# The output of the last pass is turned by VectorE in squares of 32 instead of by TensorE

## The chip, the core and the metric

The kernel runs on one core of a Trainium2 chip. The engines are TensorE (PE; its weight loads are listed as PEld), VectorE (DVE), ScalarE (ACT), GpSimd (POOL) and SyncE (SP), which issues most DMA transfers. The metric is the device time of one execution in microseconds; of before there are three runs.

## The reference

Linear attention with a softmax on both sides, and then two feed-forward blocks on its 4608 x 512 output. All inputs are float32, or float64 in the weights.

```python
q_s = softmax of q over its last axis; k_s = softmax of k over the sequence
kv  = einsum('bhsd,bhse->bhde', k_s, v)
x   = einsum('bhsd,bhde->bhse', q_s, kv)          # (8, 8, 576, 64)
x   = x.transpose(0, 2, 1, 3).reshape(4608, 512)
h   = x @ w_in;  g = h / (1 + exp(-1.702 h));      x   = g @ w_out
h   = x @ w2_in; g = h, (h + 1)**2 / 4 or 0;       out = g @ w2_out
```

The last product, g (4608 x 2048) by w2_out (2048 x 512), is the last pass of the kernel, and the one that the change is about.

## The kernel before, in words

**Products.** All four matrix products run on PE in three parts each: an operand is split into a rounded part (hi, line 107, by ACT) and the remainder (lo, line 108, by DVE), and a product is the sum of hi by hi, hi by lo and lo by hi. The last three matrix products are also cut into 2 x 2 blocks and done with seven block products instead of eight, numbered in the order `PROD = (1, 7, 6, 2, 5, 4, 3)`. Their block operands are sums of quadrants, formed by DVE (`operand` and `last_sum`, through the helper on line 121).

**The last pass** is `out_pass` with `ph = 1`. Activations stand with features on the partitions and tokens along the columns. The tokens are cut into five groups (`HALVES`); a group has two halves of 512 columns (the first three groups) or 384 (the last two). For each group and each of the seven products there are four steps i (a quarter of the sum over features); a step is 12 matmuls of 128 x 512 or 128 x 384 (line 344). `ready(s)` makes hi and lo of step s; the loop calls it three steps ahead (`LA = 3`). hi and lo rotate through seven buffers, so those of step s + 3 take the place of what step s reads.

**The end of a product** is `post`. Three PSUM tiles of two banks hold running sums: "a" (products 1 and 2), "p" (7 and 4) and "x" (a copy of the first, then 6, 5 and 3). After 1 ACT copies a to x (line 420); after 7 and 6 it copies the sum to buffers s7 and u2 (`keep`, line 407); after 2 and 3 it copies the finished blocks c11 and c12. After 5 and 4, DVE adds the sum to s7 and u2 (`more`). Each finished block is 256 output features by 512 or 384 tokens.

**Turning.** The output wants tokens on rows, so a block must be turned. `store` puts it in a list, and `turn`, called after step i = 2 of the next product, does it: eight PE transposes of 128 columns (line 367) into the fourth PSUM tile, a copy to SBUF by ACT (line 376), and one transfer whose runs in the output are 256 floats, 1 KB (line 378). The very last product is run in two halves of its output features; `close` copies each half (lines 390 and 392), and the second half is turned after the last matmul (lines 373 and 374).

**What sets the order.** Each engine takes its instructions in one fixed order. A scheduler in the framework sets it ahead of time, from its own estimates; `behind(x, y)` pins x after y on one engine without a wait. The loads of the next group's quadrants (`Quadrants.load`, line 267) are issued by SP after products 2, 5 and 4 and stand in one queue with the outputs. Quadrant "22" of the next group, loaded after product 4, is first read by the sums for product 7.

Of the kernel before, what the change touches and what calls it, by code (L numbers as in the profile page):

```python
# [8 lines left out]
FP32 = mybir.dt.float32  # L9
# [9 lines left out]
def kernel(  # L19
# [11 lines left out]
    nc = tc.nc  # L31
# [72 lines left out]
        return first  # L104

    def split(hi, lo, src):
        nc.scalar.activation(out=hi, in_=src, func=ACTF.Copy)  # L107
        return nc.vector.tensor_tensor(out=lo, in0=src, in1=hi.bitcast(FP32), op=ALU.subtract)  # L108


    def behind(ins, other):
# [12 lines left out]
    def weight_sets(width, raws, f12, f_r, f_s, hls):  # L124
        w_srcs = {"out1": w1_out, "in2": w2_in, "out2": w2_out}
        hl_n = [0]

        def raw(i):
            return raws[i % len(raws)].bitcast(I64)


        def load(w, si, i):
            src = w_srcs[w]
            if w == "in2":
                c0 = i * (DFF // 2) + si * width
# [12 lines left out]
        def convert(i):  # L148
            conv(raw(i), f12[i], f_r.bitcast(U32))

        def quads(w):
            if w == "in2":
                v4 = [f.rearrange("p (k f) -> p k f", k=KD) for f in f12]
                return v4[0][:, 0:2], v4[0][:, 2:4], v4[1][:, 0:2], v4[1][:, 2:4]
            v2 = [f.rearrange("p (c f) -> p c f", c=width // P) for f in f12]
            return v2[0][:, :, 0:256], v2[1][:, :, 0:256], v2[0][:, :, 256:512], v2[1][:, :, 256:512]

        def hl(w, si, p, src, neg=False):
            t = hls[hl_n[0] % len(hls)].bitcast(FP32R)
            hl_n[0] += 1  # L160
            t = t.rearrange("p (a c f) -> p a c f", a=2, c=src.shape[1])
            hi, lo = t[:, 0], t[:, 1]
            if neg:
                nc.scalar.activation(out=hi, in_=src, func=ACTF.Copy, scale=-1.0)
                nc.vector.scalar_tensor_tensor(
                    out=lo, in0=src, scalar=-1.0, in1=hi.bitcast(FP32), op0=ALU.mult, op1=ALU.subtract
                )
            else:
                split(hi, lo, src)
            n = 2 * width  # L170
            dst = wp_dram[w, p].rearrange("p a s f -> p a (s f)")[:, :, si * n:(si + 1) * n]
            nc.sync.dma_start(out=dst, in_=t.bitcast(FP32).rearrange("p a c f -> p a (c f)"))

        def sums(w, si, part):
            a11, a12, a21, a22 = quads(w)
            s = f_s.rearrange("p (c f) -> p c f", c=a11.shape[1])
            if part == 0:
                hl(w, si, 1, a11)
                tt(s, a21, a22, ALU.add)
            elif part == 1:  # L180
                hl(w, si, 5, s)
                hl(w, si, 4, a22, neg=True)
                tt(a21, a11, a21, ALU.subtract)
            elif part == 2:
                tt(s, s, a11, ALU.subtract)
                hl(w, si, 6, s)
                hl(w, si, 2, a12)
            else:
                hl(w, si, 7, a21)
                tt(a12, a12, s, ALU.subtract)  # L190
                hl(w, si, 3, a12)

        return load, convert, sums
# [53 lines left out]

    G_AT = ({"11": 0, "12": 4, "22": 8, "21": 12}, {"11": 0, "12": 16, "22": 4, "21": 12})
    R_AT = ((16, 17, 18, 19, 24, 25, 26), (8, 9, 10, 11, 25, 26, 24))
    O_AT = {"s7": 20, "u2": 21, "c11": 22}  # L250
    C_AT = {p: 4 + 2 * i for i, p in enumerate(PROD)}
    C_AT[PROD[-1]] = 20
    E_AT = (22, 23, 24, 25, 26)
# [46 lines left out]
    def out_pass(ph, gq, sl):  # L300
# [8 lines left out]
        def ready(s):  # L309
            if s >= len(steps):  # L310
                return
            j, p, i = steps[s]
            src, ins = operand(gq.t[j], p, i)
            if j == 0:
                behind(ins, last.get(s - 2))
            n = HALVES[j]
            if ph and s < len(first_at):
                at = first_at[s]
            elif ph and s >= len(steps) - 4:
                at = (i, 16 + i)  # L320
            else:
                k = 2 * (s - len(first_at) * ph)
                at = [r_at[(k + x) % len(r_at)] for x in range(2)]
            hi, lo = (slot(x, FP32R)[:, :, :n] for x in at)
            last[s] = split(hi, lo, src)
            ops[s] = hi, lo
            if p == 2:
                last_sum(gq.t[j], i)

        def gemm(s, ms=range(2)):  # L330
            j, p, i = steps[s]
# [16 lines left out]
                            skip_group_check=True,  # L348
                        )

        late = []

        def store(j, a, b, t):
            n, t0 = HALVES[j], STARTS[j]
            if not ph:
                nc.sync.dma_start(out=x1_dram[j, a, b], in_=t)
            else:
                late.append((j, a, b, t, (0, 1)))

        def turn():  # L360
            for j, a, b, t, ms in late:
                n, t0 = HALVES[j], STARTS[j]
                n4 = n // 4
                pt = bank(2, "pt").rearrange("p a c -> p (a c)").rearrange("p (r d) -> p r d", r=4)
                for r in range(4):
                    for m in ms:
                        nc.tensor.transpose(  # L367
                            out=pt[:n4, r, m * P:(m + 1) * P], in_=t[:, m, r * n4:(r + 1) * n4], identity=ident
                        )
                u = slot(23).rearrange("p a c -> p (a c)").rearrange("p (r d) -> p r d", r=4)  # L370
                d = slice(ms[0] * P, (ms[-1] + 1) * P)
                if ms == (1,):
                    nc.scalar.activation(out=u[:n4, :2, d], in_=pt[:n4, :2, d], func=ACTF.Copy)
                    nc.vector.tensor_copy(out=u[:n4, 2:, d], in_=pt[:n4, 2:, d])
                else:
                    nc.scalar.activation(out=u[:n4, :, d], in_=pt[:n4, :, d], func=ACTF.Copy)
                r0 = t0 + b * n
                nc.sync.dma_start(
                    out=out[r0:r0 + n, a * 256 + d.start:a * 256 + d.stop].rearrange("(r p) d -> p r d", r=4),
                    in_=u[:n4, :, d],  # L380
                )
            late.clear()


        def close(m):
            n = HALVES[-1]
            z = zs["x"][:, m, :n]
            t = tmp["c12"] = tmp["c12"] if m else slot(20)[:, :, :n]
            c = n // 2 if m else n
            nc.scalar.activation(out=t[:, m, :c], in_=z[:, :c], func=ACTF.Copy)  # L390
            if m:
                nc.vector.tensor_copy(out=t[:, m, c:], in_=z[:, c:])
            late.append((NJ - 1, 0, 1, t, (m,)))

        tmp = {}

        def post(j, p):
            n = HALVES[j]
            z = zs[Z_OF[p]][:, :, :n]

            def new(name):
                at = O_AT[name] if name in O_AT else (20 if ph else 23)
                return slot(at)[:, :, :n]

            def keep(name):
                t = new(name)
                nc.scalar.activation(out=t, in_=z, func=ACTF.Copy, scale=1.0 if ph else 0.5)
                return t

            def more(t):  # L410
                if ph:
                    tt(t, t, z, ALU.add)
                else:
                    nc.vector.scalar_tensor_tensor(
                        out=t, in0=z, scalar=0.5, in1=t, op0=ALU.mult, op1=ALU.add
# [1 line left out]

            if p == 1:
                zs["x"] = bank(3, "zx")
                nc.scalar.activation(out=zs["x"][:, :, :n], in_=z, func=ACTF.Copy)  # L420
            elif p == 7:
                tmp["s7"] = keep("s7")
            elif p == 6:
                tmp["u2"] = keep("u2")
            elif p == 2:
                store(j, 0, 0, keep("c11"))
            elif p == 5:
                more(tmp["s7"])
                store(j, 1, 1, tmp["s7"])
            elif p == 4:  # L430
                more(tmp["u2"])
                store(j, 1, 0, tmp["u2"])
            else:
                store(j, 0, 1, keep("c12"))

        LA = 3

        def run(hooks, done, first=()):
# [2 lines left out]
            whole = len(steps) - 4 * ph  # L441
            for s, (j, p, i) in enumerate(steps[:whole]):
                gemm(s)
                if i == 2 and ph:
                    turn()
                if i == 3:
                    post(j, p)
                    if j + 1 < NJ:
# [2 lines left out]
                    else:  # L451
                        for f, a in hooks.get(p, ()):
                            f(*a)
                if s + LA >= done:
                    ready(s + LA)
                if s == 3:
                    for f, a in first:
# [1 line left out]
            if ph:  # L459

                for m in range(2):
                    for i in range(4):
                        gemm(whole + i, (m,))
                        if m == 0 and i == 0:
                            ready(whole + 3)
                        if i == 2:
                            turn()
                    close(m)
                turn()

        return ready, run

# [522 lines left out]
```

## Time and profile before

| | |
|---|---|
| median of three runs | 1594.03 us |
| the three runs | 1591.33, 1594.03, 1594.37 us |
| the profiled execution: span, first to last instruction | 1588.7 us |
| the profiled execution's own device time | not recorded; the median is 5.3 us above the span |
| PE busy | 1555.3 us (98%) |
| DVE busy | 1146.4 us (72%) |
| ACT busy | 850.9 us (54%) |
| last pass | about 1241 to 1588.7 us |
| transposes on PE in the last pass | 160, from 1271.3 to 1584.0 us |
| output transfers | 21 |

The span is what the profiler sees from the first to the last instruction; the device time of a run has a few microseconds more around it. A busy share is an average over stages; the rows further down are of single stages.

### The profile page before, as it was taken

To read this page: it belongs to the slowest core of one execution; us is meant where nothing else is said; L and a number is where in the kernel's file an instruction comes from. 1 tells how busy PE (TensorE), PEld (TensorE's weight loads), DVE (VectorE), ACT (ScalarE), POOL (GpSimd) and SP (SyncE) were. 2 spreads that over 40 slices of the span, in tenths; PEclk is the share of its full clock that TensorE was granted. 3 is DMA by queue.
4 is the path that set the end of the run, shared out by engine and by line. 5 is a ranking of instruction groups with operands and counts; after the bars stand their busy time and mean duration, and the time that the engine had idled before them with its cause. 6 is when DMAs were issued, how large, how long until landed. Compare 5 with 4: busy or idle time off the path is not lost. (4 is left out here: it accounts for less than half of the span.)

```text
span 1588.7 us, 21246 instructions
## 1 busy us (share of the span) xinstructions
PE 1555.3 (98%) x7908; PEld 1324.5 (83%) x7908; DVE 1146.4 (72%) x1519; ACT 850.9 (54%) x1090; POOL 8.8 (1%) x45
## 2 busy tenths in 40 slices
PE   4999999999999999999999999999999999999998
PEld 2677888777778888888999887878999888888998
DVE  6999888788753778686677687868465776766573
ACT  5555545544532444444445787878676444444453
POOL 0000000000000000000000000000000000000000
PEclk9999999999999999999999999999999999999999
DMA  8787888887778661615368766566547853424421
GB/s 229 216 262 258 279 257 270 279 286 249 237 268 302 241 237 54 225 44 169 113 205 330 272 212 246 196 239 226 203 156 285 350 206 112 153 86 134 133 66 41
DMA packets 219272, 330.66 MB, mean 208 GB/s; under 512 B 90144, under 2 KB 163232, under 8 KB 216480
## 3 DMA queue, kind: packets, MB, share of 16 engines
q1 hardware_dynamic: 214688, 328.19, 60.8%
q10 hardware_dynamic: 4480, 1.11, 0.3%
q8 instruction: 62, 1.02, 0.3%
q14 instruction: 42, 0.34, 0.1%
HBM read 190.84 MB, written 138.41 MB: 207 GB/s over the span
## 5 line engine op out<-in xcount | busy, mean ns | idle before, releaser
L107 ACT ACTIVATE s<-s 128x1024 fp32r<-128x1024 f32 (+2 forms) x363 | 325.2, 901 | 363.7 <-PE z L344 171.3
L108 DVE TENSOR_TENSOR s<-s,s 128x1024 fp32r<-128x1024 f32 (+2 forms) x363 | 369.9, 1024 | 162.5 <-PE z L344 65.8
L344 PE MATMUL z<-s,w 128*128 128x512 f32 (+1 forms) x1920 | 402.2, 368 | 0.4 <-DVE s L108 0.4
L344 PEld LDWEIGHTS z<-s,w 128*128 128x128 f32 x1920 | 349.0, 188 | 45.6 <-DVE s L108 0.8
L344 PE MATMUL zx<-s,w 128*128 128x512 f32 (+1 forms) x1440 | 303.7, 368 | 0.6 <-ACT s L390 0.6
L344 PEld LDWEIGHTS zx<-s,w 128*128 128x128 f32 x1440 | 261.6, 188 | 34.2 <-ACT s L390 0.9
L814 PE MATMUL hps<-xh,w 128*128 128x512 f32 x576 | 236.3, 410 | 3.2 <-ACT w L107 3.2
L816 PE MATMUL hps<-xh,w 128*128 128x512 f32 x576 | 226.8, 394 | 0.6 <-DVE w L108 0.6
L815 PE MATMUL hps<-xl,w 128*128 128x512 f32 x576 | 226.1, 393 | 0.0
L121 DVE TENSOR_TENSOR s<-s,s 128x1024 f32<-128x1024 f32 (+2 forms) x196 | 205.6, 1059 | 19.7 <-DMA s<-g 14.9
L496 PE MATMUL z<-s,w 128*128 128x512 f32 (+1 forms) x960 | 207.2, 367 | 0.1
L496 PEld LDWEIGHTS z<-s,w 128*128 128x128 f32 x960 | 175.0, 188 | 23.1 <-DVE s L512 0.5
L496 PE MATMUL zx<-s,w 128*128 128x512 f32 (+1 forms) x720 | 158.6, 369 | 2.5 <-DVE s L121 2.5
L496 PEld LDWEIGHTS zx<-s,w 128*128 128x128 f32 x720 | 130.7, 188 | 22.1 <-DVE s L121 4.7
L814 PEld LDWEIGHTS hps<-xh,w 128*128 128x128 f32 x576 | 108.8, 189 | 29.0 <-ACT w L107 4.8
L824 DVE SCALAR_TENSOR_TENSOR sg<-sg,hps 128x1024 f32<-128x1024 f32 x72 | 87.7, 1218 | 61.5 <-ACT sg L823 59.7
L816 PEld LDWEIGHTS hps<-xh,w 128*128 128x128 f32 x576 | 108.2, 188 | 25.5 <-DVE w L108 2.4
L823 ACT ACTIVATE sg<-hps 128x1024 f32<-128x1024 f32 x72 | 73.9, 1026 | 102.0 <-PE hps L816 96.9
L815 PEld LDWEIGHTS hps<-xl,w 128*128 128x128 f32 x576 | 108.5, 188 | 21.0 <-issue 0.4
L511 ACT ACTIVATE s<-s 128x1024 f32<-128x1024 f32 (+1 forms) x80 | 77.6, 971 | 1.6
L510 ACT ACTIVATE s<-s,half 128x1024 f32<-128x1024 f32 (+1 forms) x40 | 42.4, 1061 | 23.3 <-DVE s L121 23.2
L512 DVE SCALAR_TENSOR_TENSOR s<-s,s 128x1024 f32<-128x1024 f32 (+1 forms) x40 | 44.7, 1117 | 12.4 <-ACT s L511 11.0
(83 smaller groups left out, 1121.0 us busy)
## 6 DMA issues: line engine op xcount, KB each, us to landing
s<-g SPq DMA_DIRECT2D x96, 512.0 KB, 4.5
g<-sg SPq DMA_DIRECT2D x72, 512.0 KB, 3.2
w<-wp_out SPq DMA_DIRECT2D x14, 2048.0 KB, 15.0
g<-s SPq DMA_DIRECT2D x48, 512.0 KB, 3.0
s<-g SPq DMA_DIRECT2D x48, 384.0 KB, 3.7
wp_out<-w SPq DMA_DIRECT2D x28, 512.0 KB, 4.0
wp_in<-w SPq DMA_DIRECT2D x28, 512.0 KB, 3.7
w<-wp_in SPq DMA_DIRECT2D x7, 2048.0 KB, 8.6
```

The lines of the kernel that those rows point to most:

```text
L107: nc.scalar.activation(out=hi, in_=src, func=ACTF.Copy)
L108: return nc.vector.tensor_tensor(out=lo, in0=src, in1=hi.bitcast(FP32), op=ALU.subtract)
L121: return nc.vector.tensor_tensor(out=o, in0=x, in1=y, op=op)
L344: nc.tensor.matmul(out=z[:, m, :n], lhsT=a, rhs=b[:, c, :], start=(p in OPENS and i == 0 and c == 0 and x == 0), stop=(i == 3 and c == 1 a ...
L496: nc.tensor.matmul(out=z[:, m, :n], lhsT=a, rhs=b[:, c, :], start=(p in OPENS and c == 0 and x == 0), stop=(c == 1 and x == 2), skip_group ...
L511: nc.scalar.activation(out=t, in_=t, func=ACTF.Square)
L512: nc.vector.scalar_tensor_tensor(out=t, in0=h, scalar=1.0, in1=t, op0=ALU.max, op1=ALU.min)
L814: nc.tensor.matmul(out=hps, lhsT=wh, rhs=xh[:, kk, :], start=(kk == 0), stop=False)
L815: nc.tensor.matmul(out=hps, lhsT=wh, rhs=xl[:, kk, :], start=False, stop=False)
L816: nc.tensor.matmul(out=hps, lhsT=wl, rhs=xh[:, kk, :], start=False, stop=(kk == KD - 1))
L823: nc.scalar.activation(out=sg, in_=hps, func=ACTF.Tanh, scale=0.851)
L824: nc.vector.scalar_tensor_tensor(out=sg, in0=sg, scalar=1.0, in1=hps, op0=ALU.add, op1=ALU.mult)
```

## The change

`turn`, `late` and `close` go. `store` now has DVE turn a block in squares of 32 x 32 into a buffer, from PSUM directly for c11 and c12, and issues four transfers, one for each 32 partitions; their runs in the output are 64 floats, 256 bytes (32 floats for the two pieces of the last product, where two of the four of the second piece are issued by ACT). So that a square's features stand side by side in the output, the columns of the last product's weights are put in another order when they are split (`hl` for "out2"); the negated split there becomes two instructions. In the loop, `ready(s + 3)` now comes ahead of `post`, and the work of `post` is pinned behind it: what ACT does behind hi, what DVE does behind lo (`after`).

```diff
     def split(hi, lo, src):
-        nc.scalar.activation(out=hi, in_=src, func=ACTF.Copy)
-        return nc.vector.tensor_tensor(out=lo, in0=src, in1=hi.bitcast(FP32), op=ALU.subtract)
+        first = nc.scalar.activation(out=hi, in_=src, func=ACTF.Copy)
+        return nc.vector.tensor_tensor(out=lo, in0=src, in1=hi.bitcast(FP32), op=ALU.subtract), first
...
+            if w == "out2":
+                hi, lo = (x.rearrange("p c (m b f) -> p (c m) b f", m=2, b=4) for x in (hi, lo))
+                src = src.rearrange("p c (b m f) -> p (c m) b f", m=2, b=4)
...
-    O_AT = {"s7": 20, "u2": 21, "c11": 22}
+    O_AT = {"s7": 20, "u2": 21, "c11": 22, "c12": 23}
+    T_AT = (22, 23)
...
+        first_of, now = {}, [None]
+
+        def after(ins, on_act=False):
+            if ph:
+                behind(ins, (first_of if on_act else last).get(now[0]))
+            return ins
...
-        def store(j, a, b, t):
+        def store(j, a, b, t, ms=(0, 1)):
...
-            else:
-                late.append((j, a, b, t, (0, 1)))
-
-        def turn():
-            for j, a, b, t, ms in late:
...
-                        nc.tensor.transpose(
-                            out=pt[:n4, r, m * P:(m + 1) * P], in_=t[:, m, r * n4:(r + 1) * n4], identity=ident
-                        )
...
+            u = slot(T_AT[n_out[0] % len(T_AT)]).rearrange("p a c -> p (a c)")[:, :g * k]
+            after(nc.vector.transpose(
+                out=u.rearrange("p (g m f) -> p m g f", g=g, f=32),
+                in_=t.rearrange("p m (g r) -> p m g r", r=32),
+            ))
+            r0 = t0 + b * n
+            for q4 in range(4):
+                eng = nc.scalar if ms == (1,) and q4 % 2 else nc.sync
+                d0 = a * 256 + q4 * 64 + ms[0] * 32
+                eng.dma_start(
+                    out=out[r0:r0 + n, d0:d0 + k].rearrange("(g r) d -> r g d", r=32),
+                    in_=u[q4 * 32:(q4 + 1) * 32].rearrange("p (g d) -> p g d", g=g),
                 )
...
-                store(j, 0, 0, keep("c11"))
+                store(j, 0, 0, z if ph else keep("c11"))
...
                 gemm(s)
-                if i == 2 and ph:
-                    turn()
+                if ph and done <= s + LA < whole + 3:
+                    ready(s + LA)
+                    now[0] = s + LA
                 if i == 3:
                     post(j, p)
...
-                    close(m)
-                turn()
+                    store(NJ - 1, 0, 1, zs["x"][:, m:m + 1, :HALVES[-1]], (m,))
```

PE, the first group, product 5, where step 2 ends and step 3 begins (zx is the PSUM tile x, s_ an hi or lo buffer). Before:

```order
L344 MATMUL zx<-s_10592,w 128x512
L344 MATMUL zx<-s_10591,w 128x512 x2
L344 MATMUL zx<-s_10592,w 128x512
L344 MATMUL zx<-s_10591,w 128x512
L367 MATMUL pt<-ident,s_10580 128x128 x8
L344 MATMUL zx<-s_10608,w 128x512
L344 MATMUL zx<-s_10609,w 128x512
```

After, the same place:

```order
L359 MATMUL zx<-s_10590,w 128x512
L359 MATMUL zx<-s_10589,w 128x512 x2
L359 MATMUL zx<-s_10590,w 128x512
L359 MATMUL zx<-s_10589,w 128x512
L359 MATMUL zx<-s_10620,w 128x512
L359 MATMUL zx<-s_10621,w 128x512
L359 MATMUL zx<-s_10620,w 128x512 x2
```

The eight transposes between the steps are gone; the matmuls stand as they did.

DVE, the change from the second group to the third (line 121 are sums of quadrants, s_11312 and s_11288 the first piece of quadrant "22"; line 108 is lo; line 377 of the changed program is the turn of c12). Before:

```order
L108 TENSOR_TENSOR s_11296<-s_10756,s_11295 128x1024
L121 TENSOR_TENSOR s_11227<-s_11312,s_11227 128x1024
L121 TENSOR_TENSOR s_11068<-s_11068,z 128x1024
L108 TENSOR_TENSOR s_11329<-s_10758,s_11328 128x1024
L121 TENSOR_TENSOR s_11229<-s_11314,s_11229 128x1024
L108 TENSOR_TENSOR s_11345<-s_10760,s_11344 128x1024
L108 TENSOR_TENSOR s_11361<-s_11140,s_11360 128x1024
L121 TENSOR_TENSOR s_11231<-s_11316,s_11231 128x1024
L121 TENSOR_TENSOR s_11140<-s_11227,s_11140 128x1024
L108 TENSOR_TENSOR s_11389<-s_11142,s_11388 128x1024
```

After:

```order
L108 TENSOR_TENSOR s_11365<-s_11133,s_11364 128x1024
L377 STREAM_TRANSPOSE s_11368<-zx 128x2x16x32
L108 TENSOR_TENSOR s_11388<-s_11135,s_11387 128x1024
L121 TENSOR_TENSOR s_11209<-s_11288,s_11209 128x1024
L121 TENSOR_TENSOR s_11129<-s_11209,s_11129 128x1024
L108 TENSOR_TENSOR s_11405<-s_11209,s_11404 128x1024
L121 TENSOR_TENSOR s_11211<-s_11290,s_11211 128x1024
L121 TENSOR_TENSOR s_11213<-s_11292,s_11213 128x1024
L121 TENSOR_TENSOR s_11215<-s_11294,s_11215 128x1024
L108 TENSOR_TENSOR s_11422<-s_11211,s_11421 128x1024
```

The turn stands behind the lo of step 2 of product 1, and the sums for product 7, which stood between the lo of product 3, now come after it, three of them in a row.

SP, the same change of group (g_2 are loads of the third group's quadrants, the two digits behind it the quadrant, the last its piece). Before, from the output of s7 on:

```order
L378 DMA out_dram<-s_11207 128x4x256
L267 DMA s_11324<-g_2102_224 128x1024
L267 DMA s_11326<-g_2103_225 128x1024
L267 DMA s_11312<-g_2110_226 128x1024
L267 DMA s_11314<-g_2111_227 128x1024
L378 DMA out_dram<-s_11292 128x4x256
L267 DMA s_11316<-g_2112_228 128x1024
L267 DMA s_11318<-g_2113_229 128x1024
L378 DMA out_dram<-s_11385 128x4x256
```

After, with the outputs of s7 and u2 in four transfers each:

```order
L385 DMA out_dram<-s_11203 32x16x64 x4
L275 DMA s_11215<-g_2013_221 128x1024
L385 DMA out_dram<-s_11282 32x16x64 x4
L275 DMA s_11288<-g_2110_226 128x1024
L275 DMA s_11290<-g_2111_227 128x1024
L275 DMA s_11292<-g_2112_228 128x1024
L275 DMA s_11294<-g_2113_229 128x1024
L275 DMA s_11296<-g_2100_222 128x1024
```

All four loads of quadrant "22" (g_211) now stand behind the outputs of u2; before, two of them did. Output transfers go from 1 to 4 a block.

## Rows read from the trace of the kernel before

**Rows 1.** The page's head: span, then an engine's busy time, share and instructions.

```profile
span 1588.7 us, 21246 instructions
...
PE 1555.3 (98%) x7908; PEld 1324.5 (83%) x7908; DVE 1146.4 (72%) x1519; ACT 850.9 (54%) x1090; POOL 8.8 (1%) x45
```

**Rows 2.** Windows: busy us and instructions of PE, PEld, DVE, ACT, POOL; clock; DMA share.

```profile
930.00:1242.00 312.00, 308.99 (x1509) 272.72 (x1508) 216.88 (x266) 230.15 (x282) 0.00 (x0) 1.00 0.63 228
1262.00:1577.60 315.60, 315.58 (x1622) 282.16 (x1620) 214.31 (x199) 153.73 (x162) 0.00 (x0) 1.00 0.38 119
1577.60:1588.70 11.10, 5.71 (x32) 4.87 (x32) 0.78 (x2) 1.81 (x5) 0.00 (x0) 0.99 0.25 71
```

**Rows 3.** The chain of waits, 1240 to 1589 us: shares, then start, length, what.

```profile
by line: PE z L344 50.8%; PE zx L344 42.2%; PE pt L367 4.9%; DMA out_dram<-s 0.6%; ACT s L376 0.2%; ACT s L390 0.1%; DVE s L374 0.1%; ACT s L373 0.1%; issue 0.1%; ACTq L373 0.0%; ACTq L376 0.0%
...
1343.00 8.16 PE zx L344 x36
...
1351.17 0.87 PE pt L367 x8
...
1475.60 8.32 PE zx L344 x48
```

**Rows 4.** Lines 367 and 378 (the latter from 1570 us): ns min/median/max, starts, landing.

```profile
L367 PE MATMUL pt<-ident,s x160: 270/272/317, 1271.3 to 1584.0; 128*128 128x128 f32 x96, 128*96 128x128 f32 x64
...
L378 SPq DMA_DIRECT2D out_dram<-s x4: 317/318/318, 1571.6 to 1585.7; - x4
...
DMA to landing us min/median/max: 2.1/2.5/3.0
```

**Rows 5.** The timeline of the end: start, length, engine, line, [idle before <- releaser].

```profile
1578.16 3.39 PE L344 MATMUL zx<-s,w 128*128 128x384 f32 x18 [0.58 <-ACT s L390]
...
1581.74 1.32 PE L344 MATMUL zx<-s,w 128*128 128x384 f32 x6
...
1585.28 0.42 DVE L374 COPY s<-pt 96x256 f32<-96x256 f32 x1 [1.47 <-ACT s L373]
```

**Rows 6.** Lines of DVE: count | busy us, mean ns of one | idle before.

```profile
L374 DVE COPY s<-pt 96x256 f32<-96x256 f32 x1 | 0.4, 421 | 1.5 <-ACT s L373 1.5
...
L392 DVE COPY s<-zx 128x192 f32<-128x192 f32 x1 | 0.4, 358 | 9.9 <-ACT s L390 9.9
...
L165 DVE SCALAR_TENSOR_TENSOR s<-s,s 128x256 fp32r<-128x256 f32 x8 | 3.4, 420 | 0.0
...
L686 DVE TENSOR_TENSOR mx<-m 128x128 f32<-128x128 f32 x32 | 9.0, 282 | 0.1
```

**Rows 7.** The timeline, DVE, two instructions back to back in the last pass.

```profile
1354.81 1.22 DVE L121 TENSOR_TENSOR s<-s,zx 128x1024 f32<-128x1024 f32 x1 [2.33 <-PE zx L344]
...
1355.95 1.22 DVE L108 TENSOR_TENSOR s<-s,s 128x1024 fp32r<-128x1024 f32 x1
```

**Rows 8.** Waits from 1262 us on: who <- whom: us in total, times, longest.

```profile
DVE s L108 <- PE z L344: 35.7, 36, 1.5
...
DVE s L121 <- DMA s<-g: 6.2, 5, 2.4
```

**Rows 9.** The page's DMA queues: packets, MB, share of 16 engines' span.

```profile
q10 hardware_dynamic: 4480, 1.11, 0.3%
```

**Rows 10.** Lines 647 (v) and 267 (last pass): issue ns, starts; us to landing.

```profile
L647 SPq DMA_DIRECT2D v<-in_v_dram x60: 548/629/2615, 9.1 to 405.4; - x60
...
DMA to landing us min/median/max: 2.8/4.0/8.6
...
L267 SPq DMA_DIRECT2D s<-g x62: 319/517/675, 1262.9 to 1515.7; - x62
...
DMA to landing us min/median/max: 3.1/3.8/7.6
```

More of the change, by code (lines that the diff above doesn't have):

```diff
@@ L162, in hl @@
             hi, lo = t[:, 0], t[:, 1]
+            if w == "out2":
+                hi, lo = (x.rearrange("p c (m b f) -> p (c m) b f", m=2, b=4) for x in (hi, lo))
+                src = src.rearrange("p c (b m f) -> p (c m) b f", m=2, b=4)
             if neg:
                 nc.scalar.activation(out=hi, in_=src, func=ACTF.Copy, scale=-1.0)
-                nc.vector.scalar_tensor_tensor(
-                    out=lo, in0=src, scalar=-1.0, in1=hi.bitcast(FP32), op0=ALU.mult, op1=ALU.subtract
-                )
+                n = 2 if w == "out2" else 1
+                for c in range(0, src.shape[1], src.shape[1] // n):
+                    r = slice(c, c + src.shape[1] // n)
+                    nc.vector.scalar_tensor_tensor(
+                        out=lo[:, r], in0=src[:, r], scalar=-1.0, in1=hi[:, r].bitcast(FP32),
+                        op0=ALU.mult, op1=ALU.subtract,
+                    )
             else:
@@ L324, in ready @@
             hi, lo = (slot(x, FP32R)[:, :, :n] for x in at)
-            last[s] = split(hi, lo, src)
+            last[s], first_of[s] = split(hi, lo, src)
             ops[s] = hi, lo
@@ L349, in gemm @@
                         )
-        late = []
-        def store(j, a, b, t):
+        n_out = [0]
+        def store(j, a, b, t, ms=(0, 1)):
             n, t0 = HALVES[j], STARTS[j]
@@ L356, in store @@
                 nc.sync.dma_start(out=x1_dram[j, a, b], in_=t)
-            else:
-                late.append((j, a, b, t, (0, 1)))
-        def turn():
-            for j, a, b, t, ms in late:
[L362 to L366, printed above, removed]
-                        nc.tensor.transpose(
-                            out=pt[:n4, r, m * P:(m + 1) * P], in_=t[:, m, r * n4:(r + 1) * n4], identity=ident
[L369 to L380, printed above, removed]
-                )
-            late.clear()
@@ L385, in close @@
[L385 to L393, printed above, removed]
+                return
+            g = n // 32
+            k = len(ms) * 32
+            n_out[0] += 1
@@ L399, in post @@
             z = zs[Z_OF[p]][:, :, :n]
-            def new(name):
-                at = O_AT[name] if name in O_AT else (20 if ph else 23)
-                return slot(at)[:, :, :n]
             def keep(name):
-                t = new(name)
-                nc.scalar.activation(out=t, in_=z, func=ACTF.Copy, scale=1.0 if ph else 0.5)
+                t = slot(O_AT[name])[:, :, :n]
+                after(nc.scalar.activation(out=t, in_=z, func=ACTF.Copy, scale=1.0 if ph else 0.5), True)
                 return t
@@ L411, in more @@
                 if ph:
-                    tt(t, t, z, ALU.add)
+                    after(tt(t, t, z, ALU.add))
                 else:
@@ L419, in post @@
                 zs["x"] = bank(3, "zx")
-                nc.scalar.activation(out=zs["x"][:, :, :n], in_=z, func=ACTF.Copy)
+                after(nc.scalar.activation(out=zs["x"][:, :, :n], in_=z, func=ACTF.Copy), True)
             elif p == 7:
@@ L433, in post @@
             else:
-                store(j, 0, 1, keep("c12"))
+                store(j, 0, 1, z if ph else keep("c12"))
         LA = 3
@@ L453, in run @@
                             f(*a)
-                if s + LA >= done:
+                if not ph and s + LA >= done:
                     ready(s + LA)
@@ L465, in run @@
                             ready(whole + 3)
-                        if i == 2:
-                            turn()
-                    close(m)
-                turn()
+                    store(NJ - 1, 0, 1, zs["x"][:, m:m + 1, :HALVES[-1]], (m,))
         return ready, run
```

## The prediction

> **What bounds the kernel now.** I read the head of the page first: PE is busy for 1555.3 of a span of 1588.7 us [rows 1]. A share over the whole program says little about one stage, so next come the stretches: in the last pass, from 1262.0 to 1577.6 us, PE is busy for 315.58 of 315.60 us at a granted clock of 1.00, while DVE is busy for 214.31 us and the DMA engines for 0.38 of the time [rows 2]. Nothing that another engine does there can shorten the pass; only work taken off PE can. The chain of waits says the same: from 1240 us on it is PE matmuls and nothing else until 1577.6 us, and 4.9% of that stretch is the transposes of line 367, which stand in the chain in pieces of eight for 0.87 us between the matmuls of a product (8.16 us of three steps, then the piece) [rows 3]. There are 160 of them [rows 4], so 19 such pieces, one of four inside the last product and one of four behind it.
>
> The end is its own stage. After the first half of the last product PE waits 0.58 us for ACT's copy of that half, and the last matmul ends at 1581.74 + 1.32 = 1583.06 us [rows 5]. Behind it come a copy shared by ACT and DVE, four transposes, a second copy that ends at 1585.70, and the last output transfer, issued at 1585.7 [rows 4]. The span ends at 1588.7, which is 5.64 us after the last matmul.
>
> **The change part by part.** *PE loses all of line 367.* In the order of the changed program the last pass has matmuls of the products alone. That is 19 x 0.873 = 16.6 us and 0.44 us for the four inside the last product, all of it on the path. It stays gained if PE is not made to wait, so the rest of the working looks for what is late next.
>
> *DVE gets 21 transposes in 32x32 squares.* The trace of before has none. The nearest rows are DVE copies out of PSUM, 358 ns for 192 columns and 421 ns for 256: 0.98 ns an element on 0.17 us, which makes 1.17 us for 1024 columns, 0.92 for 768 and 0.55 for 384 [rows 6]. An addition of 1024 columns out of PSUM took 1.22 us [rows 7]. I take 1.17; the slope alone (1.00) and the addition bound it, but the operation itself could be slower than any row, which is a rival below. [...] All 19 of the large ones add some 20 us to the 214 of 316 us.
>
> Whether they hide is a question of order. A rounding's second part ("lo", line 108) for the step three ahead starts when the step now running ends, since its buffer is the one that step read: DVE waits for PE there, 36 times at the ends of products in one pair of banks alone, 1.5 us at most [rows 8]. A step is 8.16 / 3 = 2.72 us, so lo is wanted 5.44 us after it can start. Back to back such DVE instructions follow each other in 1.14 us [rows 7]. The tie puts the transpose behind lo, never ahead of it. The tightest place is the start of the next group of tokens: after the end of product 3 DVE has lo, the transpose, lo, two sums, lo, three sums, and the lo that step 2 of product 7 wants, five steps or 13.6 us later. That is nine instructions of 1.14 us and the transpose: 10.26 + 1.17 = 11.4 us, or 11.8 with the wait for PE in between. Slack 1.8 us: hidden.
>
> *Output leaves in four transfers of 32 partitions, in runs of 256 bytes instead of 1 KB.* A store of 512 KB is then 2048 pieces. Reads in 256-byte runs are in the trace: queue q10 moved 4480 packets in 0.3% of 16 x 1588.7 us, about 17 ns each [rows 9]; 2048 of them on 16 engines are 2.2 us per store, every 10.9 us at the closest. Writes of that size are not shown. SP's issue of a 128 KB transfer in 256-byte runs took 0.55 to 0.63 us, of a full load 0.52 [rows 10], so a store occupies SP for up to 2.5 us. The queue matters where loads stand behind outputs: the four loads of the quadrant "22" that product 7 of the next group needs are behind the four outputs of u2. These go out some 3.5 us after the end of product 4 (lo, the addition, the transpose), the loads from 6 us on, and they land 3.8 us after issue in the median and 7.6 at worst [rows 10]: at the latest 13.6 us, while the sum that reads the first is reached at 10.9 + 3.9 = 14.8 us. Hidden, and DVE's present waits for such loads (6.2 us over the pass) never reached PE [rows 8].
>
> *Copies that go.* ACT loses 20 copies out of PSUM and the copies of c11 and c12; it was not the bound, so I count nothing. The banks that c11 and c12 stand in are read by DVE during the next product and written again two products later or more: nothing.
>
> *The weights of the last product get their columns in another order.* In the pass before, eight negated subtractions of 256 columns (420 ns) become two of 128 (about 282) [rows 6]: 8 x 0.14 = 1.2 us on an engine that idles for 95 of 312 us there, and PE is short of work for 3 us only [rows 2]. Nothing, with 1 us either way at the bounds.
>
> *The end.* PE must still wait between the two halves of the last product, now for the transpose of the first half: 0.55 us and a hand-over, against 0.58. After the last matmul come 0.05 + 0.55 us of transpose, then two issues each on two queues, the second of them 0.3 to 0.6 us after the first, and the landing, 2.1 to 3.0 us [rows 4] or the 4.0 of 256-byte runs [rows 10]. With 0.4 and 3.0 that is 4.05 us against 5.64: 1.6 gained, between 0.3 and 2.6.
>
> **The sum**: 16.6 + 0.44 + 1.6 = 18.6 us, a span of 1570.1. What lies around the span is 1594.03 - 1588.7 = 5.3 us by the median, so 1575.4 us. The three runs of before are 3 us apart.
>
> **The rivals.** *A: the transpose takes several times a copy.* For it: four-byte data in squares is shown by no row. Against it: every DVE row near this size lies at 1 ns an element. Below 3.3 us (13.6 - 10.26) it stays hidden. At four times the slope, 4.2 us, the tight place overruns by 0.85 us (0.6 where halves have 384 columns) at each of four changes of group, and the end grows by twice 1.1: 5.3 us less gained, 1580.7 us.
>
> *B: PE is freed but waits for the loads of "22" instead.* For it: twelve transfers now stand in one row behind product 4, the four outputs first. Against: slack of over 1 us even at the worst landing. DVE's own slack of 1.8 us comes on top, so the loads have to land 10.6 us or more after issue; each microsecond beyond counts four times, and at 15 us the whole gain is spent: 1594 us, no change.
>
> *C: slower, by the small writes.* Place: the 16 DMA engines in the last pass. They are busy for 0.38 x 315.6 = 120 us now; the pass would last 297, and the change writes 38,400 pieces, 2,400 per engine. From 177 / 2400 = 74 ns a piece on, the engines are the bound; from 82 ns on the gain is spent; at 90 ns the kernel is at 1613 us. For it: no write under 1 KB bounds the price. Against: reads of this size took 17 ns, and it needs five times that. [...]
>
> *D: the change doesn't do what it says.* The order excludes that transposes stay on PE; what is left of this is A and B.
>
> **How the numbers follow.** Forecast 0.84, A 0.08, B 0.04, C 0.04. The forecast's own bounds are gains of 17.3 and 19.7 us, with some 2 us for the spread of runs: 1572.3 to 1578.7. Taken to A, the range is 1572.0 to 1581.0. A change of 0.2%, 3.2 us, is about what a measurement of this kernel can tell from none: faster 0.92 (forecast and A), same 0.04 (B), slower 0.04 (C).
>
> **What would show it.** Right: no transpose on PE in the last pass; its products in the chain in pieces of 10.88 us (8.32 where halves have 384 columns [rows 3]) without a gap; DVE transposes of 1.1 to 1.25 us; PE idle under 1 us from 1262 us to the last product; about 4 us from the last matmul to the end. A shows as transposes over 3.3 us and PE waiting for line 108 in product 7; B as the same wait with DVE held by loads; C as a DMA share near 1 in the last pass with output packets of 70 ns or more. The forecast is wrong if PE has over 3 us of waits there, or if the time before 1240 us moves by more than 2 us.

## The result, and the profile after

The changed kernel takes 1571.4 us, the median of four runs (1570.93 to 1571.93); the kernel before, run beside it, 1592.68 us, the median of four (1591.33 to 1594.37). The ratio is 0.9866, with a 95% interval of 0.9852 to 0.988: 21 us faster. Predicted were 1575.4 us and a range of 1572.0 to 1581.0; the time lies 4.0 us under the forecast and 0.6 us under the range.

First the head of the page of the kernel after, which answers to [rows 1].

```profile
span 1569.1 us, 20971 instructions
...
PE 1536.9 (98%) x7748; PEld 1307.6 (83%) x7748; DVE 1163.6 (74%) x1546; ACT 821.9 (52%) x1058; POOL 8.8 (1%) x45
```

PE has 160 instructions fewer, all of line 367, and is busy 18.4 us less. The span is 19.6 us shorter. The windows of the kernel after (busy us and instructions of PE, PEld, DVE, ACT, POOL; clock; DMA share; GB/s) answer to [rows 2]; the first ends ahead of the last product's second half, the second begins at the last matmul's end:

```profile
1262.00:1557.00 295.00, 295.00 (x1453) 263.21 (x1452) 228.75 (x217) 126.30 (x134) 0.00 (x0) 1.00 0.42 130
1564.72:1569.10 4.38, 0.00 (x0) 0.00 (x0) 0.58 (x1) 0.00 (x0) 0.00 (x0) 0.96 0.28 47
```

PE is busy for 295.00 of 295.00 us: the pass was bound by PE and still is, with less work. DVE has taken over the turns and still idles for 66 us.

The chain of waits of the kernel after, 1236 to 1569 us (start, length, what), answers to [rows 3]:

```profile
1240.51 10.88 PE zx L359 x48
1251.39 10.88 PE z L359 x48
...
1463.89 8.32 PE zx L359 x48
...
1555.41 4.18 PE zx L359 x24
1559.59 0.02 issue
1559.61 0.59 DVE s L377
...
1560.25 4.47 PE zx L359 x24
...
1564.75 0.58 DVE s L377
```

A product of 48 matmuls is one piece of 10.88 us; before, 36 matmuls were followed by a piece of 0.87. The only wait in the last pass is the one between the halves of the last product, 0.66 us from 1559.59 to 1560.25.

DVE's lines in the last pass of the kernel after, each shape apart (count, busy us, mean ns of one, idle before):

```profile
L377 DVE STREAM_TRANSPOSE s<-s 128x1024 f32<-128x1024 f32 x6 | 7.5, 1246 | 0.2
...
L377 DVE STREAM_TRANSPOSE s<-z 128x1024 f32<-128x1024 f32 x3 | 3.7, 1244 | 0.0
...
L377 DVE STREAM_TRANSPOSE s<-zx 128x384 f32<-128x384 f32 x2 | 1.2, 583 | 6.7 <-PE zx L359 6.7
L377 DVE STREAM_TRANSPOSE s<-zx 128x768 f32<-128x768 f32 x1 | 1.0, 976 | 0.0
```

A turn of 1024 columns takes 1.24 us, out of SBUF and out of PSUM (z, zx) alike. The transfers of the output in the kernel after (line 385: issue ns min/median/max, starts; landing us min/median/max), against [rows 4]:

```profile
L385 SPq DMA_DIRECT2D out_dram<-s x82: 315/488/1670, 1266.4 to 1565.7; - x82
...
L385 ACTq DMA_DIRECT2D out_dram<-s x2: 380/432/483, 1565.4 to 1565.8; - x2
...
DMA to landing us min/median/max: 1.6/2.2/6.8
```

There are 84 for 21. They land in 2.2 us in the median, where the blocks of the last pass of before took 3.0 (line 378). The loads of quadrants (line 275, 1262 to 1560 us) land later than before, against [rows 10]:

```profile
DMA to landing us min/median/max: 3.1/4.8/10.4
```

The median was 3.8 us and the longest 7.6. The rival on loads is answered further down.

### The profile page after: what moved, and what is told of

It reads as the page before. It is cut to its first block, busy times and chain, and to the rows that moved or that the text cites. A ratio compares the mean times of both kernels' runs of the same rounds, so it can differ in the third digit from the quotient of the medians.

```text
span 1569.1 us, 20971 instructions
## 1 busy us (share of the span) xinstructions
PE 1536.9 (98%) x7748; PEld 1307.6 (83%) x7748; DVE 1163.6 (74%) x1546; ACT 821.9 (52%) x1058; POOL 8.8 (1%) x45
```

## The experiments

Three things were open: whether the 0.6 us outside the range belong to the last pass or to something else (the earlier start of the last pass, the new order of the weights' columns, the number from which the forecast started); what the two halves of the change, turn and tie, are worth each; and whether DVE and the small writes have the room that the sum gave them. The times of before beside these runs were 1591.36 us (23 runs), 1591.57 (18) and 1590.55 (13).

### The kernel before once more

No edit.

> The kernel before, unchanged, in more runs and with a second profile. Theory M (the miss lies in the starting point, not in the change): the profiled execution of before was one of the fast ones, its own time its span and about 1.8 us, and executions of before scatter; so here each run's time minus its span is 1.7 to 1.9 us, spans run from 1588 to 1593 us, and the median lies at 1591 to 1594 us. Rival S (the change gains 2 to 3 us more than PE's work, outside the last pass): every run of before has a span of 1591 to 1592 us and the last pass starts 2 to 3 us later than in the changed kernel in every profile.

Measured: 1591.26 us (12 runs, 1588.06 to 1596.42), ratio 1.0 [0.9989, 1.001]. Its profiled execution took 1592.4 us with a span of 1590.6. The chain at the start of the last pass, of the kernel before and then of this run of the same program:

```profile
1241.51 4.53 PE zx L344 x20
```

```profile
1243.34 2.72 PE zx L344 x12
```

One program reaches the same matmul, the first of product 6 in the first group, 1.8 us apart. The kernel after came there at 1240.51, 1.0 us earlier than before's profiled run: inside this scatter. In the twelve profiles of this document it starts between 1239.56 and 1243.34 us where PE does the transposes (four profiles), and between 1238.55 and 1242.48 where DVE does (eight). Rival S, 2 to 3 us in every profile, falls. And around the span lie 1592.4 - 1590.6 = 1.8 us, not 5.3. The spans of the twelve runs go from 1586.2 to 1594.6 us, wider than M had them.

### The old order of the weights' columns

```diff
-            if w == "out2":
-                hi, lo = (x.rearrange("p c (m b f) -> p (c m) b f", m=2, b=4) for x in (hi, lo))
-                src = src.rearrange("p c (b m f) -> p (c m) b f", m=2, b=4)
...
-                n = 2 if w == "out2" else 1
+                n = 1
```

Taken out of the changed kernel; the output's columns then stand in another order.

> The changed kernel with the weights of the last product in their old column order and the negated split in one instruction (the output's columns are then in the wrong places). M: as the changed kernel, 1571.4 within 0.8 us, since that work is hidden in the pass before. S: 1 to 3 us slower than the changed kernel, and the last pass starts later by as much.

Measured: 1570.97 us (5 runs), ratio 0.9884 [0.9867, 0.99]. As the kernel after: the new order of columns, and the eight subtractions that became two each, cost and give nothing that can be seen.

### Each PE transpose done twice

```diff
-                        nc.tensor.transpose(
-                            out=pt[:n4, r, m * P:(m + 1) * P], in_=t[:, m, r * n4:(r + 1) * n4], identity=ident
-                        )
+                        for _ in range(2):
+                            nc.tensor.transpose(
+                                out=pt[:n4, r, m * P:(m + 1) * P], in_=t[:, m, r * n4:(r + 1) * n4], identity=ident
+                            )
```

In the kernel before.

> The kernel before with each transpose on PE done twice, all else as it was. M: a piece of eight costs the path 0.87 to 0.90 us, so 19 pieces and the four behind the first half add 17.0 to 17.5 us, and the last four behind the end another 0.2 to 0.5: 17.5 us slower than before, about 1609 to 1611 us. A rival that transposes are partly hidden (PE queue, weight loads beside matmuls): under 12 us slower.

Measured: 1607.19 us (4 runs), ratio 1.0117 [1.0094, 1.014], which is 15 to 22 us more. The chain of this run:

```profile
1344.55 8.16 PE zx L344 x36
1352.71 1.75 PE pt L368 x16
```

The piece is 1.75 us where it was 0.87 [rows 3]; 19 x 0.88 = 16.7 us. The time is 2 us below the 1609 to 1611 that were expected, but in the profiled execution product 6 of the first group starts at 1239.56 us and the span ends at 1604.0: 364.4 us for 347.2 before (1588.7 - 1241.51), 17.2 more. The price of the transposes is what the prediction read off the chain.

### The turn without the tie

```diff
-            if ph:
-                behind(ins, (first_of if on_act else last).get(now[0]))
...
-                if ph and done <= s + LA < whole + 3:
-                    ready(s + LA)
-                    now[0] = s + LA
...
-                if not ph and s + LA >= done:
+                if s + LA >= done:
```

Taken out of the changed kernel: `ready(s + 3)` comes after `post` as before, and nothing is pinned.

> The changed kernel without the tie: the work at a product's end is not pinned, and the operands of the step three ahead are made after it, as before. M: the slack of 1.8 us holds either way, so within 0.8 us of the changed kernel, 1571 to 1572 us, PE without a gap in the last pass. Rival T (the tie is what keeps the transposes off the path): PE waits for line 108 after each product's end, 0.5 to 1 us at 20 places, 10 to 20 us slower than the changed kernel.

Measured: 1590.85 us (10 runs), ratio 1.0006 [0.9994, 1.0018]. The transposes are off PE, and the whole gain is gone. M, which expected no effect, is wrong by 19 us; T has the size but not the place, since PE waits only around the four changes of group, and for ACT as well. The waits in the last pass of this run (who <- whom: us, times, longest):

```profile
ACT zx L409 <- PE z L357: 35.5, 4, 10.0
...
PE z L357 <- ACT s L107: 7.4, 4, 2.1
...
PE z L357 <- DVE s L108: 4.9, 6, 1.1
...
PE zx L357 <- ACT s L107: 1.5, 2, 0.8
```

ACT stands four times for up to 10 us at line 409, the copy of product 1's sum to x. Its order at the change from the second group to the third, in this kernel (zx is x, s_11205 to s_11209 are the sums of quadrants for product 7's first three steps):

```
L107 ACTIVATE s9_11387<-s3_11130 128x1024
L409 ACTIVATE zx_11437<-z_11374 128x1024
L107 ACTIVATE s11_11404<-s16_11205 128x1024
L107 ACTIVATE s26_11421<-s17_11207 128x1024
L107 ACTIVATE s8_11440<-s18_11209 128x1024
```

and in the kernel after (the same three are s_11209 to s_11213, the copy is line 411):

```
L107 ACTIVATE s9_11387<-s3_11135 128x1024
L107 ACTIVATE s11_11404<-s16_11209 128x1024
L107 ACTIVATE s26_11421<-s17_11211 128x1024
L107 ACTIVATE s8_11438<-s18_11213 128x1024
L411 ACTIVATE zx_11442<-z_11374 128x1024
```

The copy reads the sum that product 1 has only finished at its end. Where it stands ahead of the three roundings, product 7 begins with no operand ready. The timelines of the run show it at the first change of group (start, length, instruction, idle before): ACT, and then PE.

```profile
1303.87 1.01 ACT L409 ACTIVATE zx<-z 128x1024 f32<-128x1024 f32 x1 [10.04 <-PE z L357]
1304.79 1.05 ACT L107 ACTIVATE s<-s 128x1024 fp32r<-128x1024 f32 x1
```

```profile
1305.89 0.50 PE L357 MATMUL z<-s,w 128*128 128x512 f32 x1 [2.06 <-ACT s L107]
1307.15 4.62 PE L357 MATMUL z<-s,w 128*128 128x512 f32 x12 [0.76 <-DVE s L108]
```

In the order of the kernel before the copy stood behind those roundings without a pin, with a copy of the turn (line 376) among them, which waits for PE's transposes (13.7 us in all from 1262 to 1577 us). That this copy is why the scheduler had it so was not tried. That the place decides is shown by the next pair of runs. PE's waits for roundings add up to 7.4 + 4.9 + 1.5 = 13.8 us here; the rest of the loss lies behind these waits, part of it in a lower granted clock (0.50 at the first change of group, last section).

### One half of the tie at a time

Two kernels, each the changed one with one of the pins: ACT's alone, and DVE's alone.

```diff
-            if ph:
-                behind(ins, (first_of if on_act else last).get(now[0]))
+            if ph and on_act:
+                behind(ins, first_of.get(now[0]))
```

```diff
-            if ph:
-                behind(ins, (first_of if on_act else last).get(now[0]))
+            if ph and not on_act:
+                behind(ins, last.get(now[0]))
```

> The changed kernel with only ACT's half of the tie (copies at a product's end behind hi), DVE's half left out. Theory P (what the unpinned version lost was one ACT copy, a to x after product 1, standing ahead of three roundings for product 7 and waiting there for PE): as the changed kernel, 1570 to 1573 us, and no gap on PE at the end of product 1. Rival Q (DVE's half matters as well, the turn must not stand ahead of lo): 2 to 10 us slower, with PE waiting for line 108.

> The changed kernel with only DVE's half of the tie. P: the same gaps as without any tie, some 4 to 6 us at the end of product 1 in each of four groups, 1588 to 1592 us. Q: most of the gain comes back, under 1580 us.

Measured: ACT's pin alone 1571.11 us (4 runs), ratio 0.9876 [0.9857, 0.9894]; DVE's alone 1591.63 (10 runs), ratio 0.9998 [0.9988, 1.0009]. The window 1262 to 1557 us of the first, and of the second:

```profile
1262.00:1557.00 295.00, 295.00 (x1451) 263.05 (x1450) 228.69 (x217) 126.46 (x134) 0.00 (x0) 1.00 0.42 130
```

```profile
1262.00:1557.00 295.00, 283.97 (x1334) 246.79 (x1334) 215.23 (x203) 120.92 (x128) 0.00 (x0) 0.98 0.41 127
```

With DVE's pin alone PE idles 11 us there and ACT's copy waits 35.5 us in all, as without any tie:

```profile
ACT zx L411 <- PE z L359: 35.5, 4, 10.0
```

Both kernels have the loop's new order, so that order and DVE's pin together give nothing; ACT's pin without the new order was not run. What the tie is worth is the place of the instructions that ACT's pin moves, and line 411 is the one that ACT is seen to wait at.

### The tie without the turn

The kernel before with `first_of`, `after` and the loop's new order as in the diff of the change; the transposes stay on PE.

> The kernel before with the tie alone: ready(s + 3) ahead of post, ACT's and DVE's work of post pinned behind the rounding; the 160 transposes stay on PE, the output leaves as before. Theory P (the tie only keeps PE fed once the transposes have left it; by itself there is nothing to win, since PE was busy for 315.58 of 315.60 us in the last pass of before): 1591.4 us, within 1.5 of the kernel before, PE without a gap in the last pass. Rival G (the tie is worth something by itself, and the changed kernel's gain is the sum of two): 1585 to 1589 us. Rival L (pinning the copies behind the rounding makes PE's turn in the next product late, because the copy that feeds it comes later): 1593 to 1597 us, with PE waiting at line 367.

Measured: 1591.3 us (10 runs), ratio 1.0006 [0.9996, 1.0016]. PE is busy for 314.65 of 315 us from 1262 us on:

```profile
1262.00:1577.00 315.00, 314.65 (x1618) 281.44 (x1616) 213.81 (x198) 154.03 (x163) 0.00 (x0) 1.00 0.36 118
```

By itself the tie gives nothing; it and the turn make one change.

### The turn four times, and twice

```diff
-            after(nc.vector.transpose(
+            for _ in range(4 if len(ms) == 2 else 1):
+              after(nc.vector.transpose(
```

The 19 large turns of the changed kernel; in a second kernel, 2 in place of 4.

> The changed kernel with each of the 19 large turns on DVE done four times over. By the prediction's slack (a turn may last 3.3 us before the ninth instruction behind it is late) a turn of 4.6 us overruns by 1.3 us where halves have 512 columns and 1.0 to 2.0 us in the later groups, at the four changes of group: 5 to 6 us slower than the changed kernel, about 1577 us, and PE's waits at product 7 only. Rival: 57 more turns of 1.15 us that are not hidden, 65 us slower; or all hidden, no difference.

> The changed kernel with each of the 19 large DVE turns done twice (2.48 instead of 1.24 us). In the order as built the turn of c12 stands behind the lo of product 1's step 3 at the change from the first group to the second, and ahead of it at the later ones. Theory F (room counted along the order as built): behind that lo the chain is 2.72 us of waiting, lo, turn, two sums, lo, three sums, lo = 2.72 + 8 x 1.14 + 1.24 = 13.1 us of 13.6, so 0.5 us of room there and some 1.9 at the other changes; 1.24 more overruns by 0.7 us once: 1572 to 1573 us, PE waiting for line 108 only at the first change of group. Rival N (no room anywhere, each turn's extra 1.24 us is paid at each of the four changes, as the run with four turns would have it if spread evenly): 1575.5 to 1577 us. Rival H (room for 3.3 us at each change, as the prediction counted): 1571.4 us, no wait of PE.

Measured: four times, 1587.76 us (9 runs), ratio 0.9977 [0.9967, 0.9987]; twice, 1573.07 us (4 runs), ratio 0.9889 [0.9874, 0.9904]. DVE's timeline of the kernel after at the change from the second group to the third, and of the run with four turns:

```profile
1371.16 1.23 DVE L108 TENSOR_TENSOR s<-s,s 128x1024 fp32r<-128x1024 f32 x1 [1.48 <-PE zx L359]
1372.31 1.24 DVE L377 STREAM_TRANSPOSE s<-zx 128x1024 f32<-128x1024 f32 x1
1373.88 1.23 DVE L108 TENSOR_TENSOR s<-s,s 128x1024 fp32r<-128x1024 f32 x1 [0.33 <-issue]
1375.02 2.48 DVE L121 TENSOR_TENSOR s<-s,s 128x1024 f32<-128x1024 f32 x2
1377.46 1.23 DVE L108 TENSOR_TENSOR s<-s,s 128x1024 fp32r<-128x1024 f32 x1
1378.60 3.49 DVE L121 TENSOR_TENSOR s<-s,s 128x1024 f32<-128x1024 f32 x3
```

```profile
1374.70 1.23 DVE L108 TENSOR_TENSOR s<-s,s 128x1024 fp32r<-128x1024 f32 x1 [0.34 <-PE zx L359]
1377.42 1.23 DVE L108 TENSOR_TENSOR s<-s,s 128x1024 fp32r<-128x1024 f32 x1 [1.49 <-PE z L359]
1378.57 5.09 DVE L378 STREAM_TRANSPOSE s<-zx 128x1024 f32<-128x1024 f32 x4
```

The chain of the run with four turns, where product 1 starts and where product 6 does:

```profile
1374.60 2.73 PE z L359 x12
...
1400.04 2.04 PE zx L359 x9
```

In the kernel after DVE goes through the tight place as the prediction listed it. With four turns the scheduler put them one lo later, behind that of product 1's step 3, so DVE first stands 1.49 us for PE, and then for 5.09 us at the turns. Products 1 and 7, 21.76 us together in the kernel after, took from 1374.60 to 1400.04 us, 3.7 us more: about the length of the three added turns (5.09 - 1.24 = 3.85 us). Some 4 us at each of the four changes make the 16. The 5 to 6 us that were expected took the order as given, and the scheduler changed it: a turn of another length is also a turn in another place.

In the kernel after the turn stands behind that lo at the first change of group alone. Counted along this order the chain is 13.1 us of 13.6. With two turns it has to overrun there and nowhere else. PE's waits of the run with two turns, and the place of the first in PE's timeline:

```profile
PE z L359 <- DVE s L108: 0.8, 1, 0.8
PE zx L359 <- DVE s L378: 0.7, 1, 0.7
...
1310.03 8.23 PE L359 MATMUL z<-s,w 128*128 128x512 f32 x35 [0.80 <-DVE s L108]
```

One wait of 0.8 us, at the first change of group, and the usual one at the end: theory F. The time, 1573.07 us, is at the upper end of F's 1572 to 1573. The room at the first change is 1.24 - 0.8 = 0.4 us, not the 1.8 of the prediction; at the others it is more than what was added (1.24 us, 0.98 in the shorter halves).

### Writes of 128 bytes

```diff
-                eng.dma_start(
-                    out=out[r0:r0 + n, d0:d0 + k].rearrange("(g r) d -> r g d", r=32),
-                    in_=u[q4 * 32:(q4 + 1) * 32].rearrange("p (g d) -> p g d", g=g),
-                )
+                for h in range(len(ms)):
+                    eng.dma_start(
+                        out=out[r0:r0 + n, d0 + h * 32:d0 + h * 32 + 32].rearrange("(g r) d -> r g d", r=32),
+                        in_=u[q4 * 32:(q4 + 1) * 32].rearrange("p (g d) -> p g d", g=g)[:, :, h * 32:h * 32 + 32],
+                    )
```

In the changed kernel: eight transfers a block, in runs of 128 bytes.

> The changed kernel with outputs in runs of 128 bytes and twice as many transfers (eight a block). M: SP issues for 3.6 us a block instead of 1.9, the loads behind the outputs of u2 start 1.7 us later and still land in time: 0 to 2 us slower than the changed kernel. Rival C (small writes cost the DMA engines several times a read of the same size): the engines or the loads become the bound, 10 us or more slower, PE waiting for sums that wait for loads.

Measured: 1571.67 us (4 runs), ratio 0.9881 [0.9864, 0.9897]. The window of this run:

```profile
1262.00:1557.00 295.00, 295.00 (x1450) 262.92 (x1449) 228.69 (x218) 126.50 (x135) 0.00 (x0) 1.00 0.48 130
```

The DMA share goes from 0.42 to 0.48 and PE has no wait in this window: twice as many pieces of half the size leave room still.

## Why the prediction was right in its mechanism and wrong in its time

**The sum of the span held.** Predicted was a gain of 18.6 us: 16.6 for the 19 pieces, 0.44 inside the last product, 1.6 at the end. From the start of product 6 of the first group to the end of the span the kernel before takes 1588.7 - 1241.51 = 347.2 us, the kernel after 1569.1 - 1240.51 = 328.6: 18.6 us. The repeat of before has 1590.6 - 1243.34 = 347.3 and the run with the old columns 1568.4 - 1239.63 = 328.8, so this holds from one execution to the next. That it fits to the tenth is luck: 17.3 us were gained up to the last matmul where the sum has 16.6 + 0.44, and 1.3 behind it where it has 1.6. The other 1.0 us of the span's 19.6 came ahead of the last pass, in the scatter that the profiles show.

**The step that failed is the last line of the sum**, "What lies around the span is 1594.03 - 1588.7 = 5.3 us by the median". It set a median of three runs beside the span of an execution whose own time wasn't known. In every run whose time and span are both known, 1.7 to 2.0 us lie between them, 1.8 in most and never 5.3 (1570.93 and 1569.1, 1592.4 and 1590.6). So that execution took about 1590.5 us, and 1594.03 was a high one: 54 later runs gave medians of 1590.55 to 1591.57. From 1590.5 the same sum gives 1571.9, within the four runs measured (1570.93 to 1571.93) and 0.5 us over their median. The spread of the three runs was put into the range as a scatter around 1594, when it was a doubt about the starting point; one of the three was at 1591.33. What stays open is some 1 us: between the medians of later runs of before (1591.36) and of the changed kernel (1571.4) lie 20 us, and the sum has 18.6. The last pass does not hold it, and single executions of one program lie further apart than that.

**The end** was forecast at 4.05 us behind the last matmul; it is 4.38, against 5.64 before: 1.3 us gained for 1.6. The terms named there add up to 4.00, not 4.05. The turn took 0.58 us, and the second issue came 0.4 after the first; that transfer landed after 2.1 us, not 3.0, and the span ended some 1.2 us behind its landing, which the sum has no term for. So two errors nearly cancel. The turn of the first half made PE wait 0.66 us, where the copy had made it wait 0.58.

**The turn's length** was 1.24 us for 1.17, 0.98 for 0.92 and 0.58 for 0.55. From 384 to 1024 columns the rows rise by 1246 - 583 = 663 ns, 1.04 ns a column. Rival A, a turn over 3.3 us, falls.

**The room on DVE** was read from one change of group, the second, and called the tightest. The order at the first is tighter by a lo that waits for PE. The slack of 1.8 us was 0.4 there; that the turn stayed hidden all the same was luck. The last lo of the list is the one that step i = 1 of product 7 wants (step 2 counted from 1); the 13.6 us are right for it. The 36 waits of [rows 8] are at the ends of steps, not of products, of which those banks have 20.

**The tie was given no price.** The prediction used it only to say where the turn stands. Without ACT's part of it there is no gain at all, the expectation of the run without the tie missed that once more, and the sentence on ACT, "it was not the bound, so I count nothing", was right only since the pin holds the copy back: an engine with half its time free (ACT is busy for 126.30 of 295.00 us in the kernel after) can still stand in the wrong place. The order of the changed program did show the copy behind the roundings; what it would do elsewhere was not asked.

**Rival B** (the loads of "22") does not show: PE has no wait for them. But its ground holds in part. The longest landing of a load rose from 7.6 to 10.4 us, past what the prediction took as the worst and close to the 10.6 us from which it let the loads be late. The four loads of "22" are the first of eight in a row behind the outputs of u2, and in the kernel after they landed 6.5 us after issue at the latest; the 10.4 us are of the last of a row, which is not a load of "22".

**Rival C** falls. Between the kernel after and the run with 128-byte pieces the queue's row (packets, MB, share of 16 engines, 1262 to 1570 us) goes from the first line to the second:

```profile
q1 hardware_dynamic: 52256, 38.71, 41.2%
q1 hardware_dynamic: 88800, 38.71, 46.9%
```

That is 5.7% of 308 us on 16 engines for some 36,500 more packets and the same bytes, about 8 ns each. And the share of the last pass was 0.42 in the kernel after for 0.38 before [rows 2], 124 us for 120: 256-byte pieces in place of 1 KB cost some 4 us of the engines' time, where C needed 177. In the packet records of its last pass a 256-byte packet took 16.4 ns in the mean, far from 74 and close to the 17 that the prediction took from reads. (At 90 ns the prediction's terms give about 1614 us, not 1613.) Between pieces of 256 and of 128 bytes the device time shows no difference: 1571.4 and 1571.67 us.

**Rival D** falls: no transpose is left on PE. That the turn without the tie leaves the time as it was is none of the four rivals.

## What to carry to other kernels

Take the time of the profiled execution itself as the starting point, by span plus the constant that other runs show, and treat a median of three runs with a spread of 3 us as a guess, here wrong by 3.5 us. When work leaves a bound engine, ask of every other engine in order what it waits at and what is queued behind that; a fixed order can give back the whole gain through one copy on an engine that is half idle (here 1590.85 us for 1571.4). Count the room of a moved instruction at every place where it occurs, since a scheduler may set each of them differently, and may set them anew when an instruction's length changes.

## What the runs showed of the hardware

TensorE's granted clock fell to 0.50 after some of the waits. In the run without the tie PE stood for 2.06 us at the first change of group, did one matmul and stood for another 0.76 us. Windows of that run there, and at the third change (columns as in the windows above):

```profile
1306.00:1307.00 1.00, 0.39 (x1) 0.07 (x1) 1.00 (x1) 0.00 (x0) 0.00 (x0) 1.00 0.00 0
1308.00:1310.00 2.00, 2.00 (x6) 1.51 (x6) 2.00 (x3) 1.60 (x2) 0.00 (x0) 0.50 0.00 0
1311.00:1313.00 2.00, 1.26 (x6) 0.73 (x5) 1.77 (x2) 1.60 (x2) 0.00 (x0) 1.00 0.00 0
...
1465.00:1475.00 10.00, 6.70 (x36) 5.80 (x35) 7.79 (x9) 5.45 (x7) 0.00 (x0) 1.00 0.03 7
```

At the first change the granted clock went from 1.00 to 0.50 and back to 1.00. The twelve matmuls behind the wait took 4.62 us; in the run with four turns twelve of the same size took 3.00 us behind a wait of 0.76 us, at a granted clock of 1.00:

```profile
1307.43 3.00 PE L359 MATMUL z<-s,w 128*128 128x512 f32 x12 [0.76 <-DVE s L108]
```

By these two the lower clock cost about 4.62 - 3.00 = 1.6 us there, an estimate, on top of the waits. Not every such wait is followed by it: at the third change of the run without the tie PE stood for 1.63, 0.55 and 1.12 us, and the granted clock stayed at 1.00.

In the kernel after, a turn of 128 x 1024 float32 in 32x32 squares took DVE about what an addition of that size did: 1246 ns from SBUF and 1244 from PSUM (z), against 1219 and 1213. Between 1262 and 1557 us a transfer of 128 KB in 256-byte runs landed in 2.4 us in the median in the kernel after, where one of 512 KB in 1 KB runs took 3.2 in the kernel before.
